# Cosine attention and a gated MLP on one core: three-chunk score visits, a Newton norm for one unit, and a new order of early loads

## The chip, the cores and the metric

The kernel runs on one core of one Trainium2 chip. The metric is the device time of one execution in microseconds (us). Profiles are of single executions; a core has five engines with a queue each: TensorE (PE, with its weight loads as PEld), VectorE (DVE), ScalarE (ACT), GpSimd (POOL) and SyncE (SP, which here only issues DMAs).

## What is computed

The reference, cut to what matters (8 batches, 12 heads, 448 positions, head width 64; 3584 tokens, model width 768, hidden width 2048):

```python
q_n = q / (norm(q, axis=-1) + 1e-06)
k_n = k / (norm(k, axis=-1) + 1e-06)
scores = matmul(q_n, k_n.T) / tau              # tau = 0.1
attn = exp(scores - max(scores)); attn = attn / sum(attn)
x = matmul(attn, v)                            # heads joined: 3584 x 768
h = x @ w_in                                   # 768 x 2048
g = h * cos(h)
out = g @ w_out                                # 2048 x 768
```

All inputs and the output are float32 in DRAM; the kernel multiplies in bfloat16.

## The kernel before, in words

**Units and groups.** The work is cut into 16 units of six heads (two units are one batch) and 48 groups of two heads (three groups are one unit, six a batch, PB = 6). Group g belongs to unit u = g // 3.

**One unit's inputs** (`load` L647, `load_v` L655, `copy_v` L665, `norms` L933). SP issues the DMAs of k and q (both into a `raw` buffer, two buffers, units alternate) and of v (`vin`). `square` (L680) squares 112x1024 elements a group, on POOL unless `PLAN` (L14) or the rule in `norms` names ACT or DVE; `reduce` (L696) sums on DVE; `rnorm` (L704) makes 1/norm on ACT as exp(-0.5 ln x), for one group in units 0 and 1 and for three groups at once afterwards; `scale` (L714) multiplies k and q by it, on POOL except for group 0. `copy_v` casts v to bfloat16, on DVE for units 0 and 1 and on POOL afterwards.

**One group's attention.** `transposes` (L730) turns the normed k and q so that the head width lies on partitions: on TensorE and then a DVE copy for groups below `BYPE` = 9, by a DMA transpose from SP above. `scores` (L756) makes one of four chunks of scores: two matmuls, one a head, each on half of the array's rows, into one of two PSUM tiles SC0 and SC1 (two banks each); ACT takes the exponential of the chunk (PX). `both` (L950) puts two chunks together; such a run of score matmuls, between matmuls that use all rows, is called a visit here. `attend` (L776) multiplies PX by v into the PSUM tile AV, and DVE takes the reciprocal of the sums (`rcp`) and scales (`xs`, both read AV). xs is transposed into xT: by DMA, or, for the groups in `XPE` (batch 0 and the last group of each batch), by TensorE into the AV tile (XP) and a DVE copy.

**The MLP.** `m1` (L815) is the first projection of one batch: eight steps of 24/2 matmuls of 448 columns, into SC0, SC1 and AV in the order of `TURN`; the last step lies in AV. ACT takes the cosine (as a sine, for which it loads another table, 1.28 us each way) and DVE multiplies (gT). `m2_emit` (L866) is the second projection in halves of 16 matmuls of 384 columns, into PSUM tiles PO and PO2 in turn, then a DVE copy (osb) and an output DMA. PO2 is also the tile of the transposes (TP).

**What sets the order.** The code only lists operations with costs; a planner (`play` L218, `arrange` L176) plays them through and writes each engine's fixed order; `pick` (L264) chooses for TensorE among the first three groups of stream A and the head of stream B, which holds M2 alone and fills. Operations with a bias over 500 (the weight loads) are taken by their due times `DUE` (L522), W1.0 at -20, W1.1 at 10, W2.0 to W2.3 at 20, 24, 28, 32. W1 is loaded in halves and W2 in quarters by DMAs that POOL issues (`load_w1` L906, `load_w2` L912). Where TensorE would idle early, dummy matmuls on zeros (L919) are put in.

**The main sequence** (L981 to L1041): norms and transposes of group 0; groups 0 to 5 by `pair` (L956); loads of unit 2, W2.0 and W2.1, the norms of unit 2, loads of unit 3 after W1.1 has landed; transposes of groups 6 to 8; `m1(0)`; then groups 6 to 47 by `pair`, with `m1(b)` and its M2 after group 6(b+1)+1 (after group 12 for b = 1), and `m1(7)` and the rest of M2 at the end. M2 of the next to last batch is listed with eight halves only, the rest after the last attend.

## Time and profile before

| what | value |
|---|---|
| median of 6 runs | 434.8 us (433.85 to 435.63) |
| the profiled execution | 435.49 us |
| its span in the profile | 433.6 us |
| granted TensorE clock | 1.0 throughout |
| ACT exponentials (L767) | 192, 165.0 us busy, 914 ns each |
| M2 (L877), M1 (L826), AV (L785), scores (L762) on PE | 816+64+16, 480+288, 1536, 384 matmuls |
| POOL squares (L693) and scales (L719) | 42 and 47, 1906 and 1903 ns each |
| DMA queues: SP and ACT / POOL | 55.6% / 7.9% of 16 engines' span |

How to read it: a matmul's end is modelled, so that pieces of work are best measured from one start to the next; the projection's 24 matmuls take 4.54 us in the chain of waits. The first 36 us hold the attention of batch 0, 36.5 to 56.4 the first projection, 56.4 to 90.9 attention with the first M2; from 109.5 on attention with M2 and projections follow in turn, and from 397.6 only M2 is left.

### The profile page before, as it was taken

To read this page: it belongs to the slowest core of one execution; us is meant where nothing else is said; L and a number is where in the kernel's file an instruction comes from. 1 tells how busy PE (TensorE), PEld (TensorE's weight loads), DVE (VectorE), ACT (ScalarE), POOL (GpSimd) and SP (SyncE) were. 2 spreads that over 40 slices of the span, in tenths; PEclk is the share of its full clock that TensorE was granted. 3 is DMA by queue.
4 is the path that set the end of the run, shared out by engine and by line. 5 is a ranking of instruction groups with operands and counts; after the bars stand their busy time and mean duration, and the time that the engine had idled before them with its cause. 6 is when DMAs were issued, how large, how long until landed. Compare 5 with 4: busy or idle time off the path is not lost.

```text
span 433.6 us, 8767 instructions
## 1 busy us (share of the span) xinstructions
PE 417.9 (96%) x3756; PEld 225.8 (52%) x3756; DVE 212.9 (49%) x297; ACT 264.6 (61%) x319; POOL 192.8 (44%) x118
## 2 busy tenths in 40 slices
PE   7889999999899999999999989999999999999996
PEld 2455545544555545555555545555555545655663
DVE  5776646464636356534853366424853344335221
ACT  3887386874777647784677637774677547734000
POOL 3995167912876546932496056921596000000000
PEclk9999999999999999999999999999999999999999
DMA  9999997598179596648757694759857102200322
GB/s 230 264 246 213 241 273 160 143 234 211 33 176 244 105 266 188 107 117 224 180 118 115 164 232 95 122 133 211 176 113 134 48 0 59 59 2 0 100 81 77
DMA packets 94631, 63.87 MB, mean 147 GB/s; under 512 B 55040, under 2 KB 89600, under 8 KB 94592
## 3 DMA queue, kind: packets, MB, share of 16 engines
q1 hardware_dynamic: 90064, 56.16, 55.6%
q0 software_dynamic: 3680, 6.29, 7.9%
q10 hardware_dynamic: 848, 0.86, 0.7%
q8 instruction: 30, 0.49, 0.5%
q14 instruction: 9, 0.07, 0.1%
HBM read 45.61 MB, written 11.01 MB: 131 GB/s over the span
## 4 chain that ended last, share of the span: by engine, by line
PE 79%; ACT 7%; issue 5%; POOL 3%; DMA 3%; DVE 2%; SPq 0%; POOLq 0%; ACTq 0%
PE PO L877 29%; PE SC L826 16%; PE AV L785 10%; PE AV L826 10%; PE SC L762 9%; ACT PX L767 6%; DMA raw<-in_q_dram 3%; PE SC L877 2%; POOL sq L693 2%; POOL qks L719 1%; PE AV L877 1%; DVE n L700 1%; DVE gT L842 1%; ACT cosb L840 0%; PE PO L745 0%
## 5 line engine op out<-in xcount | busy, mean ns | idle before, releaser
L767 ACT ACTIVATE PX<-SC 112x896 bf16<-112x896 f32 x192 | 165.0, 914 | 44.3 <-PE SC L762 43.8
L877 PE MATMUL PO<-W,gT 128*128 128x384 bf16 x816 | 148.6, 326 | 0.0
L693 POOL TENSOR_TENSOR sq<-raw 112x1024 bf16<-112x1024 f32 x42 | 79.4, 1906 | 103.4 <-DMA raw<-in_q_dram 103.4
L877 PEld LDWEIGHTS PO<-W,gT 128*128 128x128 bf16 x816 | 73.0, 97 | 56.8 <-issue 13.1
L719 POOL TENSOR_TENSOR qks<-raw,rn 112x1024 bf16<-112x1024 f32 x47 | 88.4, 1903 | 25.0 <-ACT rn L711 25.0
L826 PE MATMUL SC<-xT,W 128*128 128x448 bf16 x480 | 95.5, 352 | 1.0 <-ACT PX L767 1.0
L842 DVE TENSOR_TENSOR gT<-SC,cosb 128x896 bf16<-128x896 f32 x40 | 43.5, 1091 | 54.9 <-ACT cosb L840 54.6
L840 ACT ACTIVATE cosb<-SC,cst 128x896 f32<-128x896 f32 x40 | 40.2, 1007 | 48.4 <-PE SC L826 43.4
L826 PEld LDWEIGHTS SC<-xT,W 128*128 128x128 bf16 x480 | 46.6, 98 | 43.9 <-issue 1.4
L700 DVE TENSOR_REDUCE n<-sq 112x16 f32<-112x1024 bf16 (+1 forms) x49 | 58.1, 1191 | 16.8 <-POOL sq L693 12.0
L826 PE MATMUL AV<-xT,W 128*128 128x448 bf16 x288 | 58.7, 352 | 2.4 <-ACT cosb L840 1.2
L762 PE MATMUL SC<-qkT 64*128 64x448 bf16 x384 | 55.5, 355 | 5.0 <-ACT PX L767 2.2
L785 PEld LDWEIGHTS AV<-va,PX 112*128 112x128 bf16 x1536 | 49.4, 97 | 15.6 <-issue 11.3
L785 PE MATMUL AV<-va,PX 112*128 112x65 bf16 x1536 | 54.8, 193 | 0.9 <-ACT PX L767 0.8
L884 DVE COPY osb<-PO 128x384 f32<-128x384 f32 x51 | 28.2, 553 | 39.2 <-PE PO L877 39.2
L840 ACT ACTIVATE cosb<-AV,cst 128x896 f32<-128x896 f32 x24 | 24.2, 1007 | 33.9 <-PE AV L826 33.8
L826 PEld LDWEIGHTS AV<-xT,W 128*128 128x128 bf16 x288 | 27.5, 98 | 30.1 <-ACT cosb L840 2.6
L794 DVE RECIPROCAL rcp<-AV 112x8 f32<-112x8 f32 x48 | 10.0, 207 | 66.5 <-PE AV L785 66.5
L842 DVE TENSOR_TENSOR gT<-AV,cosb 128x896 bf16<-128x896 f32 x24 | 26.2, 1090 | 18.7 <-ACT cosb L840 18.6
L795 DVE TENSOR_TENSOR xs<-AV,rcp 112x512 bf16<-112x512 f32 x48 | 33.2, 692 | 2.0
L762 PEld LDWEIGHTS SC<-qkT 64*128 64x128 bf16 x384 | 13.3, 94 | 37.6 <-ACT PX L767 17.4
L667 POOL CAST va<-vin 112x1536 bf16<-112x1536 f32 x14 | 20.5, 1465 | 11.1 <-DMA vin<-in_v_dram 7.7
(34 smaller groups left out, 121.9 us busy)
## 6 DMA issues: line engine op xcount, KB each, us to landing
vin<-in_v_dram SPq DMA_DIRECT2D x16, 672.0 KB, 10.9
raw<-in_k_dram SPq DMA_DIRECT2D x12, 672.0 KB, 8.4
raw<-in_q_dram SPq DMA_DIRECT2D x12, 672.0 KB, 10.7
W<-in_moe_w_in_dram POOLq DMA_DIRECT2D x2, 1536.0 KB, 14.6
W<-in_moe_w_out_dram POOLq DMA_DIRECT2D x4, 768.0 KB, 21.4
raw<-in_k_dram SPq DMA_DIRECT2D x12, 224.0 KB, 7.1
out_dram<-osb SPq DMA_DIRECT2D x7, 336.0 KB, 2.8
out_dram<-osb SPq DMA_DIRECT2D x8, 288.0 KB, 2.7
```

The source lines that it names most:

```text
L693: pool(lambda e, x=x, y=y: e.tensor_tensor(y, x, x, ALU.mult), src_, dst, 0.1 + n * 1.78e-3, label="sq%d.%d" % (u, p))
L700: dve(lambda e, w=w: e.tensor_reduce(out=n2v[i][:, 2 * p : 2 * p + 2, w], in_=sqv[p][:, :, w, :], axis=mybir.AxisListType.X, op=ALU.add), ...
L719: f = lambda e, s0=s0, s1=s1: e.tensor_tensor(qksv[i][:, p, s0:s1, :, :].rearrange("p s h d -> p h s d"), rawv[i][:, h, s0:s1, :], bass.AP ...
L762: t = e.matmul(SCv[z][:, a, 0:S], qkT[k].ap()[r, NP * c : NP * c + 128], qkT[k].ap()[r, S : 2 * S], start=True, stop=True)
L767: act(lambda e: e.activation(PXv[j][:, c, 0 : 2 * S].rearrange("p (a s) -> p a s", a=2), SCv[z][0:NP, :, 0:S], ACT.Exp, scale=1.0 / TAU), ...
L785: t = e.matmul(AVv[:, a, DV * x : DV * x + n], PXv[j][:, c, k : k + 128], vav[i][:, NJ * (2 * p + a) + c, 0:n], start=(c == 0), stop=(c == ...
L795: dve(lambda e: e.tensor_tensor(xsv[y].rearrange("p x h d -> p h x d"), AXv[:, :, :, 0:D], bass.AP(rcp[y], 0, [[NS, NP], [NJ, 2], [1, NJ], ...
L826: t = e.matmul(ph[:, a, 0:S], W1v[:, c, 128 * n : 128 * n + 128], xTv[b % 2][:, c, :], start=(c == 0), stop=(c == NKC - 1))
L840: act(lambda e, ph=ph, cz=cz: e.activation(cosv[cz], ph[:, :, 0:S], ACT.Sin, bias=cst.ap()[:, 0:1], scale=1.0), names(gi) + ["cst0"], [("c ...
L842: dve(lambda e, ph=ph, cz=cz, gi=gi: e.tensor_tensor(gTv[:, 2 * gi : 2 * gi + 2, S * (b % 2) : S * (b % 2) + S], ph[:, :, 0:S], cosv[cz], ...
L877: r = e.matmul(po[:, 0:HW], gTv[:, y, col : col + 128], W2v[:, y, HW * hf : HW * hf + HW], start=(y == 0), stop=(y == NF - 1))
L884: dve(lambda e, po=po, o=o, hf=hf: e.tensor_copy(osb[o].ap()[:, HW * hf : HW * hf + HW], po[:, 0:HW]), keys, [("osb", o, hf)], HW, label=" ...
```

## The change

The visits of groups 12 to 47 hold three chunks that follow one another across groups: twelve chunks of three groups make four visits. The chunks' PSUM tile rotates over AV, SC0 and SC1. A projection stands after the second visit of a batch's first three groups. XP moves from the AV tile to PO or PO2. Unit 2's loads wait for the landing of W1.0; its squares are all on POOL, and its inverse norms are found by three Newton steps (two small DVE and twelve small POOL operations a call, two calls) in place of Ln and Exp on ACT. Its norms and transposes are listed behind `m1(0)`. Both W1 loads are issued behind sq0.2, all W2 loads behind scale1.2. Group 3's squares (unit 1) go from POOL to ACT; Ln and Exp of units 0 and 1 get a due time 4 us earlier. Groups 9 to 11 are transposed on TensorE, into AV. DVE copies v of units 0 and 1 in three pieces; group 0's two reductions become one. In the planner, a DMA from POOL is taken to start later, M2 of a second half may start while the first waits, the trials differ, and M2 is listed as five or six halves after each projection and the rest after XP.

The core of the diff:

```diff
-    "sq": ["AD", "A", "P", "P", "P", "P"],
+    "sq": ["AD", "A", "P", "A", "P", "P"],
...
-            if fill and left[fill[0].idx] == 0:
-                o = fill[0]
-                t = max(free["PE"], ready_at[o.idx])
+            o = None
+            for x in fill[:9]:
+                if left[x.idx] == 0 and (x is fill[0] or x.group != fill[0].group):
+                    y = max(free["PE"], ready_at[x.idx])
+                    if o is None or y < t - 0.15:
+                        o, t = x, y
+            if o is not None:
...
-                queue[e].append([o, o.start + (1.7 if e == "POOL" else 1.1), o.bulk + 0.02])
+                queue[e].append([o, o.start + (5.0 if e == "POOL" else 1.1), o.bulk + 0.02])
...
-    BYPE = 9
+    BYPE = 12
...
+    NEWTON, STEPS = (2,), 3
+    SQ2 = "PPP"
+    SOON = -4.0
+    BYHEAD = False
+    BEHIND0 = "sq0.2"
+    LASTW = "scale1.2"
+    BEFORE2 = "W1.0"
+    G3 = 12
+    KEEP = (0, 1, 0, 1, 0, 1, 0)
+    SPREAD = (5, 6, 6, 6, 6, 6, 6)
+    AT, AT1 = 1, 1
...
+        if u in NEWTON:
...
+            small(lambda e: e.tensor_scalar(m, m, 1e-12, None, ALU.add), km, km, dve)
+            small(lambda e: e.tensor_scalar(y.bitcast(I32), m.bitcast(I32), -0.5, 1597463007.0, ALU.mult, ALU.add), km, ky, dve)
+            for x in range(STEPS):
+                small(lambda e: e.tensor_tensor(t, y, m, ALU.mult), km + ky, kt)
+                small(lambda e: e.tensor_tensor(t, t, y, ALU.mult), kt + ky, kt)
+                small(lambda e: e.tensor_scalar(t, t, -0.5, 1.5, ALU.mult, ALU.add), kt, kt)
+                small(lambda e: e.tensor_tensor(y, t, y, ALU.mult), kt + ky, ky)
+            return
...
+        if g >= PB + UP - 1:
+            views, keys = (AVt, AVt), ("AV", "AV")
...
     def scores(g, c):
-        j, k, z = g % 2, g % UH, (c + 1) % 2
+        j, k, q = g % 2, g % UH, NJ * g + c
+        name, bank = PHs[1 + (c + 1) % 2 if g < G3 else q % 3]
...
+        keys, view = ["PO"], POv
+        if g >= 2 * PB - 1:
+            keys, view = [(["PO"], POv), ([("TP", 0), ("TP", 1)], TPv)][nhalf[0] % 2]
+            nhalf[0] += 1
...
+        if g >= 2 * PB - 1:
+            m2_emit(max(0, len(m2_queue) - KEEP[g // PB - 1]))
...
+    def visit(g, n):
+        q = NJ * g + 3 * n
+        for x in range(q, q + 3):
+            scores(x // NJ, x % NJ)
...
+    P.order_only(find(BEHIND0), find("W1.0"))
+    P.order_only(find(BEHIND), find("W1.1"))
+    last_scale = find(LASTW)
     for p in range(UP):
         load(2, p, p + 1)
+        if BEFORE2:
+            after(P.ops[-1], find(BEFORE2))
     load_w2(0)
+    P.order_only(last_scale, P.ops[-1])
...
+    for g in range(G3, NG, 3):
+        for n in range(4):
+            if n < 3:
+                ahead(g + n)
+            grouped(visit, g, n)
+            if n < 3 and g + n > PB:
+                attend(g + n - 1)
+            if n == 0:
+                values(g)
+            if g % PB == 0 and g > PB and n == (AT if g > 2 * PB else AT1):
+                project(g // PB - 1, g)
```

`ahead`, `values` and `project` hold what `pair` and the main loop held before: the next unit's norms and DMA transposes, the cast of v with the loads of unit 4, and a projection with the loads and M2 that follow it.

## The prediction, made before the changed kernel was run

> **What bounds the kernel now.** The page comes first: TensorE's share of the span and the chain of waits.
>
> ```profile
> PE 417.9 (96%) x3756; PEld 225.8 (52%) x3756; DVE 212.9 (49%) x297; ACT 264.6 (61%) x319; POOL 192.8 (44%) x118
> ...
> q0 software_dynamic: 3680, 6.29, 7.9%
> ...
> PE 79%; ACT 7%; issue 5%; POOL 3%; DMA 3%; DVE 2%; SPq 0%; POOLq 0%; ACTq 0%
> ```
>
> TensorE holds 79% of the chain and no other engine more than 7%. Next, busy time by stretch tells where it is the bound: two five-microsecond slices near the start, one projection, and the attention stretch after it.
>
> ```profile
> 55.00:60.00 5.00, 4.42 (x26) 1.99 (x24) 3.14 (x3) 3.13 (x4) 3.66 (x2) 1.00 1.11 297
> 60.00:65.00 5.00, 4.50 (x52) 2.41 (x54) 1.90 (x3) 5.00 (x7) 2.96 (x3) 1.00 1.11 256
> ...
> 145.01:164.50 19.49, 18.89 (x100) 9.52 (x98) 10.19 (x11) 8.51 (x9) 9.39 (x6) 1.00 0.95 215
> 164.50:193.76 29.26, 29.26 (x345) 16.32 (x345) 14.35 (x24) 23.48 (x30) 19.72 (x11) 1.00 0.59 130
> ```
>
> Columns: stretch, length, then busy time and count on PE, PEld, DVE, ACT and POOL, the clock, DMA share, GB/s. From 164.5 TensorE has no idle time at all (29.26 of 29.26), with ACT at 80%. So a stretch of attention is shortened only by giving TensorE less to do. What it does there is seen in the timeline of TensorE, one period:
>
> ```profile
> 221.19 0.55 PE L762 MATMUL SC<-qkT 64*128 64x448 bf16 x4
> 221.67 2.12 PE L877 MATMUL PO<-W,gT 128*128 128x384 bf16 x12
> 223.73 0.55 PE L762 MATMUL SC<-qkT 64*128 64x448 bf16 x4
> 224.21 1.14 PE L785 MATMUL AV<-va,PX 112*128 112x65 bf16 x32
> 225.19 0.81 PE L877 MATMUL PO<-W,gT 128*128 128x384 bf16 x4
> 225.94 0.55 PE L762 MATMUL SC<-qkT 64*128 64x448 bf16 x4
> ```
>
> I read starts, since ends are modelled. A visit of two score chunks lasts 0.48 (221.19 to 221.67). Its four matmuls run two at a time on halves of the array's rows; 448 columns cost 0.189 each in the projection (24 in 4.54 us in the chain), so 0.38 is work and 0.10 is not. Twelve M2 matmuls take 2.06 (221.67 to 223.73); in the tail 72 take 11.70, that is 1.95 for twelve, so another 0.11 lies between M2 and the next visit. One visit costs about 0.21 beyond its work.
>
> Early in the run TensorE does idle, and fills holes with dummy matmuls (L919):
>
> ```profile
> 56.92 2.12 PE L877 MATMUL PO<-W,gT 128*128 128x384 bf16 x12
> 58.88 0.54 PE L919 MATMUL PO<-zt 128*128 128x448 bf16 x2
> 60.20 0.36 PE L762 MATMUL SC<-qkT 64*128 64x448 bf16 x2 [0.78 <-ACT PX L767]
> 60.50 0.36 PE L919 MATMUL PO<-zt 128*128 128x448 bf16 x1
> 61.01 0.36 PE L762 MATMUL SC<-qkT 64*128 64x448 bf16 x2
> ...
> 62.11 0.82 PE L877 MATMUL PO<-W,gT 128*128 128x384 bf16 x4
> ```
>
> From 58.88 to 62.11 only three single-chunk visits of 0.30 (the third at 61.82) are real work: 2.3 us lost. A second hole lies at 89.38 to 90.94 (1.5), a third at 109.8 to 111.0 (1.2, score bank still read by a delayed gT product).
>
> [...] the DMA share is 1.0 or above until 65 us, whichever queue issues, so moving a load moves only its turn.
>
> **Part by part.**
>
> *Three-chunk visits, groups 12 to 47.* 36 groups now have 72 visits and will have 48. 24 x 0.21 = -5.0 us. Both ends: zero if the visits cannot come in time, -5.8 at 0.24 a visit.
>
> They add a wait. Chunks now rotate over AV, SC0 and SC1, and the first chunk of every visit lies in the AV bank that the AV product also uses. So a visit waits until xs of the last product has read AV, and the product waits for the first exponential of the visit. Prices from the timeline by engine:
>
> ```profile
> 171.21 0.55 PE L762 MATMUL SC<-qkT 64*128 64x448 bf16 x4
> 171.61 1.73 ACT L767 ACTIVATE PX<-SC 112x896 bf16<-112x896 f32 x2 [0.78 <-PE SC L762]
> 171.69 1.02 PEld L785 LDWEIGHTS AV<-va,PX 112*128 112x128 bf16 x32 [0.37 <-DVE osb L884]
> ...
> 172.87 0.21 DVE L794 RECIPROCAL rcp<-AV 112x8 f32<-112x8 f32 x1 [1.58 <-PE AV L785]
> 173.11 0.69 DVE L795 TENSOR_TENSOR xs<-AV,rcp 112x512 bf16<-112x512 f32 x1
> ```
>
> Visit to first exponential 0.40, one exponential 0.865, AV start to the end of xs 2.11. A visit whose product needs its first chunk repeats after 0.40 + 0.865 + 2.11 + 0.1 = 3.5; the third of four, whose product needs two new chunks, after 4.35; the fourth, with no product behind it, after three exponentials, 3.05. Four visits: 14.4. After a projection the last product sits in AV, so the first visit comes some 2.4 late (gT ends at 166.8, M1 at 164.5). From projection to projection, eight visits: 2.4 + 4.35 + 3.05 + 3.5 + 3.5 + 4.35 + 3.05 + 3.5 + 2.1 until SC0 is read = 29.8. TensorE's own demand with 100 M2 matmuls, as now, is 29.3 - 4 x 0.21 = 28.5, and 30.4 with all 112 of a batch; the tail holds 12.5 halves (200 matmuls from 397.6), seven of them the last batch's, so 5.5 halves can be drawn forward. The wait is thus covered by M2, barely. Behind a waiting visit on TensorE stands the next M2, which the planner can put first; behind a late xs on DVE stand osb copies and a 1.21 reduction. I charge +1.0 for all six stretches; bounds 0 and +10 (below).
>
> *XP to PO or TP banks, M2 spread, M2 allowed to start in the other bank.* XP's work stays (0.2 each, one a batch); its copy of 0.39 borrows an M2 bank while the other fills. Zero. Allowing the second half's M2 while the first waits is what fills 58.88 to 62.11: -2.0 of 2.3. If W2 has not landed it is 0. The four W2 issues (0.78 each) now follow scale1.2 in a row, from about 28.5, and the last comes near 31 instead of 32.16; queue q0 needs 7.9% of 433.6 = 34 us of all engines for both weights either way, so I take their landing as unchanged. At 90 and 110 I take -0.5 each, of 1.5 and 1.2.
>
> *First attention (ACT-bound, exponentials 10.04 to 35.49).* sq1.0 goes from POOL (1.9) to ACT (1.06), where 1.53 of idle time before 15.80 covers it. POOL's scales come up to 1.9 earlier; W2.0 and W2.1 (1.51 of issue at 26.10) leave scale1.2's way, which started at 27.64 though its square sums were ready before 26.3; Ln and Exp of the norms go ahead of exponentials. ACT's idle times that this can remove are 0.61, 0.79 and 0.40; I take -0.7, bounds 0 and -1.8. The value copies in three pieces, 0.58 each at the reduction's rate, cost DVE two more starts: zero.
>
> *Unit 2.* Its raw loads wait for W1.0 to land, which was 10.65 + 17.0 = 27.7 and comes sooner without them beside it, about 24. Then they share engines with W1.1: 1.34 MB, at 230 GB/s 5.9 alone, about twice that shared, so 30 to 36. POOL then has three squares (5.7), a DVE reduction (1.2), twelve Newton operations [...], two scales (3.8): transposable by 50 at worst. The first projection runs to about 55.7 and hides this; the cover of 6 us is gone at 0.75 us per operation. The second chain and scale2.2 end near 55. ACT loses a square, Ln and Exp (1.66 together) and can load its table earlier, but the first sine waited for TensorE (41.09), so zero. Behind unit 2 on POOL stand sq3.0 and sq3.1, whose data landed only at 56.3: free unless Newton runs over. Unit 3's transposes (groups 9 to 11) go from DMA to TensorE: 3 x 0.40 (45.07 to 45.46 for one, about) = +1.2.
>
> Sum: -5.0 + 1.0 - 2.0 - 1.0 - 0.7 + 1.2 = -6.5. The profiled execution took 435.49 (span 433.6, 1.9 around it), 0.69 above the median of 434.8. So its counterpart is 429.0, and the median **428.3**.
>
> **Rivals.**
> - *Everything hides*: -5.0, -1.8, -2.3, -1.5, -1.2, the 1.23 that M1 waits at 257.6 as well, +1.2: -11.8, 423.0. For: every one of these is idle time in the trace. Against: each is someone's wait, and the next wait is close.
> - *Only the visits pay*: the early holes stay because W2 or the last gT sets them, Newton operations cost 0.75 and push sq3 by 1 to 2: -5.0 + 1.2 + 1.5 = -2.3, 432.5. For: DMA is full until 65.
> - *Slower: the AV bank becomes the loop.* If two reductions of 1.21 fall before rcp or xs in each stretch, the 29.8 becomes 32.2 against 30.4 of demand: 1.8 idle x 6 = +10.8 in place of 1.0, so 434.8 - 7.5 + 10.8 = 438.1. It decides from 31.6 a stretch. For: DVE runs 14.35 of 29.26 there, and today's visits never touch AV. Against: ACT and DVE orders are planned, and M2 covers 0.6.
> - *The change does not do what it says*: the planner splits the visits again; within 0.2% of now.
>
> **Numbers.** Forecast (426 to 431) 0.42; everything hides 0.18; only the visits 0.17; slower 0.19; none 0.04. No change means within 0.2%, 0.9 us, about what this measurement can tell. Faster 0.77, same 0.04, slower 0.19. Range 422.0 to 434.5: it leaves out some 0.16 above and 0.04 below.
>
> **What would show it.** Six score matmuls per visit, and visits about 0.67 to 0.69 long; 29.2 between projections with 104 to 112 M2 matmuls in it, or PE idle before L762 put down to DVE xs (then the slower rival); no L919 at 59 to 62; POOL's small operations at 0.15 to 0.3 and scales of unit 2 done before 55. I am wrong if TensorE idles behind AV for more than 1.3 us a stretch, or if unit 2's transposes come after M1 has ended.

## The result and the profile after

The changed kernel takes 435.22 us (median of 35 runs, 433.11 to 438.87); the kernel before takes 434.54 (72 runs, 432.46 to 437.69). The ratio is 1.0021, with a 95% interval of 1.0008 to 1.0034: slower by about 0.2%, 0.9 us, where 6.5 us less were forecast, and outside the range by 0.7. The profiled execution, 433.11 us with a span of 431.3, is the fastest of the 35; a second one of the same kernel, 434.26 with a span of 432.5, lies nearer to the median, and both are used below. The profiles alone would make the changed kernel the faster one: the profiled execution of the kernel before (435.49) was above its median, both of the changed kernel are below theirs. So the result is read from the medians, and the traces are read for where time is lost and gained.

One thing sets the runs of the changed kernel apart. Of the 36 that are listed with their clock, 24 have a mean granted clock of 0.996 or less and a median of 436.1, the other twelve 0.998 or more and a median of 434.1. Of the kernel before's 161 runs in the jobs of the experiments, 19 are of the first kind.

The page first, with TensorE's share and the chain of waits:

```profile
PE 417.7 (97%) x3779; PEld 228.9 (53%) x3779; DVE 216.9 (50%) x307; ACT 262.0 (61%) x317; POOL 197.8 (46%) x142
...
q0 software_dynamic: 3680, 6.29, 7.8%
...
PE 86%; ACT 5%; DVE 3%; POOL 3%; issue 1%; DMA 1%; DVEq 0%
```

TensorE still bounds, now with 86% of the chain. The busy time by slice (columns as before: slice, length, busy time and count of PE, PEld, DVE, ACT and POOL, clock, DMA share, GB/s):

```profile
55.00:60.00 5.00, 4.04 (x36) 2.26 (x34) 2.65 (x4) 3.96 (x4) 4.27 (x11) 1.00 1.10 247
60.00:65.00 5.00, 4.63 (x32) 2.12 (x32) 3.35 (x4) 3.65 (x6) 5.00 (x4) 1.00 0.77 209
143.08:161.70 18.62, 18.52 (x98) 9.45 (x99) 10.23 (x10) 7.49 (x8) 8.88 (x5) 1.00 0.97 212
161.70:192.60 30.90, 30.83 (x356) 17.46 (x355) 13.95 (x23) 22.94 (x30) 19.64 (x11) 1.00 0.58 132
```

Between 55 and 65 TensorE isn't busier than before (8.67 us of 10 against 8.92), and GpSimd (POOL) is busy for 9.27 of the 10 where it was 6.62. The attention stretch is full, as before, and longer since it holds more M2 matmuls. TensorE's timeline there, one group of three:

```profile
263.25 0.36 PE L817 MATMUL AV<-qkT 64*128 64x448 bf16 x2
263.45 0.54 PE L817 MATMUL SC<-qkT 64*128 64x448 bf16 x4
263.92 1.47 PE L937 MATMUL PO<-W,gT 128*128 128x384 bf16 x8
265.43 1.14 PE L840 MATMUL AV<-va,PX 112*128 112x65 bf16 x32
...
270.53 0.36 PE L817 MATMUL AV<-qkT 64*128 64x448 bf16 x2
270.73 0.54 PE L817 MATMUL SC<-qkT 64*128 64x448 bf16 x4
271.21 0.82 PE L937 MATMUL PO<-W,gT 128*128 128x384 bf16 x4
271.91 1.14 PE L840 MATMUL AV<-va,PX 112*128 112x65 bf16 x32
```

The visits hold three chunks and last 0.68 (270.53 to 271.21), as forecast. But a product (AV) no longer follows a visit: it follows M2. Eight M2 matmuls at the tail's rate of 0.1625 are 1.30; the product starts 1.51 after they do (263.92 to 265.43), and in the shorter piece 0.70 after four that cost 0.65.

In the second profile of the same kernel, TensorE's timeline where the first projection hands over to attention again:

```profile
57.19 0.55 PE L799 MATMUL PO<-ident,qks 112*128 112x112 bf16 x8 [0.66 <-DVE gT L905]
57.68 0.55 PE L817 MATMUL SC<-qkT 64*128 64x448 bf16 x4
58.16 0.82 PE L937 MATMUL PO<-W,gT 128*128 128x384 bf16 x4
61.74 0.55 PE L799 MATMUL AV<-ident,qks 112*128 112x112 bf16 x8 [2.75 <-POOL qks L767]
62.22 0.36 PE L817 MATMUL SC<-qkT 64*128 64x448 bf16 x2
62.52 1.37 PE L937 MATMUL PO<-W,gT 128*128 128x384 bf16 x4
```

The fourth line is the transposing of group 8, unit 2's last, and it stands 2.75 us for GpSimd's scale (1.33 in the first profile). Four M2 matmuls behind it take 1.30 (62.52 to 63.82) instead of 0.65: the clock was lowered. In slices of five microseconds:

```profile
55.00:60.00 5.00, 3.33 (x29) 1.60 (x26) 2.34 (x3) 3.95 (x4) 4.27 (x12) 1.00 1.11 266
60.00:65.00 5.00, 3.26 (x20) 1.23 (x21) 2.15 (x3) 1.50 (x2) 5.00 (x3) 0.77 0.80 213
65.00:70.00 5.00, 5.00 (x55) 2.55 (x54) 3.22 (x5) 4.77 (x8) 3.43 (x4) 0.89 1.05 268
```

In slices of one microsecond the clock is 0.83, 0.50, 0.50, 0.50 and 0.97 from 62 to 67, with TensorE busy throughout: that loses another 1.7, as 0.23 x 5 + 0.11 x 5 does. A loss of 1.7 in 432 is a mean clock of 0.996, what most runs of this kernel show. Two waits for gT, 0.59 and 0.66, which the first profile doesn't have, come ahead of the one for group 8.

I call the time from the start of one projection to that of the next a stretch, and take 0.1625 for each M2 matmul off its length, since the two kernels place M2 differently. So cleared, the first stretch is 38.8 in the kernel before and 43.6 in the second profile of the changed one. Of these 4.8, 1.46 is work moved forward (two score chunks and a product more) and 1.4 the transposes of groups 9 to 11, which went by DMA before: some 1.9 are lost. The second stretch falls from 35.0 to 32.0, so by 1.6 without the moved work. The next four are 32.0, 31.5, 32.6 and 31.5 before and four times 31.3 after; from the third projection to the end the changed kernel gains 1.9, of which 1.1 is a single wait before a projection (1.23 at 258.8 in the kernel before).

### The profile page after: what moved, and what is told of

The parts are those of the page before. It is cut to its first block, busy times and chain, and to the rows that moved or that the text cites. A ratio compares the mean times of both kernels' runs of the same rounds, so it can differ in the third digit from the quotient of the medians.

```text
span 431.3 us, 8851 instructions
## 1 busy us (share of the span) xinstructions
PE 417.7 (97%) x3779; PEld 228.9 (53%) x3779; DVE 216.9 (50%) x307; ACT 262.0 (61%) x317; POOL 197.8 (46%) x142
## 4 chain that ended last, share of the span: by engine, by line
PE 86%; ACT 5%; DVE 3%; POOL 3%; issue 1%; DMA 1%; DVEq 0%
PE PO L937 32%; PE SC L889 19%; PE AV L889 11%; PE AV L840 11%; PE SC L817 6%; ACT PX L822 4%; PE AV L817 3%; DVE n L728 1%; POOL qks L767 1%; PE AV L937 1%; PE SC L937 1%; DMA raw<-in_q_dram 1%; DVE qks L767 1%; PE PO L870 1%; PE AV L799 0%
## 5 line engine op out<-in xcount | busy, mean ns | idle before, releaser
L937 PE MATMUL PO<-W,gT 128*128 128x384 bf16 x832 | 152.2, 327 | 0.0
L822 ACT ACTIVATE PX<-SC 112x896 bf16<-112x896 f32 x144 | 123.2, 917 | 8.5 <-PE SC L817 8.2
L937 PEld LDWEIGHTS PO<-W,gT 128*128 128x128 bf16 x832 | 74.2, 98 | 62.7 <-issue 20.0
L822 ACT ACTIVATE PX<-AV 112x896 bf16<-112x896 f32 x48 | 44.0, 917 | 47.3 <-PE AV L817 47.3
L903 ACT ACTIVATE cosb<-SC,cst 128x896 f32<-128x896 f32 x40 | 40.1, 1006 | 51.0 <-PE SC L889 51.0
L889 PEld LDWEIGHTS SC<-xT,W 128*128 128x128 bf16 x480 | 46.3, 98 | 43.6 <-issue 1.6
L728 DVE TENSOR_REDUCE n<-sq 112x16 f32<-112x1024 bf16 x48 | 57.7, 1211 | 7.0 <-POOL sq L722 4.0
L889 PE MATMUL AV<-xT,W 128*128 128x448 bf16 x288 | 58.5, 352 | 0.7
L840 PE MATMUL AV<-va,PX 112*128 112x65 bf16 x1536 | 56.2, 193 | 1.2 <-ACT PX L822 0.6
L817 PE MATMUL SC<-qkT 64*128 64x448 bf16 x288 | 41.9, 352 | 2.0 <-ACT PX L822 1.1
L905 DVE TENSOR_TENSOR gT<-AV,cosb 128x896 bf16<-128x896 f32 x24 | 26.2, 1090 | 15.1 <-ACT cosb L903 14.8
```

The costliest lines, as they stand in the source:

```text
L728: dve(lambda e, o=o, hs=hs: e.tensor_reduce(out=n2v[i][:, o, :], in_=sqv[p][:, hs[0] : hs[-1] + 1, :, :], axis=mybir.AxisListType.X, op=AL ...
L817: t = e.matmul(bank[:, a, 0:S], qkT[k].ap()[r, NP * c : NP * c + 128], qkT[k].ap()[r, S : 2 * S], start=True, stop=True)
L822: act(lambda e: e.activation(PXv[j][:, c, 0 : 2 * S].rearrange("p (a s) -> p a s", a=2), bank[0:NP, :, 0:S], ACT.Exp, scale=1.0 / TAU), [n ...
L840: t = e.matmul(AVv[:, a, DV * x : DV * x + n], PXv[j][:, c, k : k + 128], vav[i][:, NJ * (2 * p + a) + c, 0:n], start=(c == 0), stop=(c == ...
L889: t = e.matmul(ph[:, a, 0:S], W1v[:, c, 128 * n : 128 * n + 128], xTv[b % 2][:, c, :], start=(c == 0), stop=(c == NKC - 1))
L903: act(lambda e, ph=ph, cz=cz: e.activation(cosv[cz], ph[:, :, 0:S], ACT.Sin, bias=cst.ap()[:, 0:1], scale=1.0), names(gi) + ["cst0"], [("c ...
```

## The experiments

All times are medians, and the ratio is to runs of the kernel before in the same job.

| run | us | ratio | 95% interval |
|---|---|---|---|
| e1_again | 435.90 | 1.0042 | 1.0022 to 1.0062 |
| e2_after_two | 440.90 | 1.0151 | 1.0105 to 1.0196 |
| e3_before_three | 441.66 | 1.0171 | 1.0140 to 1.0202 |
| e4_after_race | 435.22 | 1.0027 | 1.0007 to 1.0047 |
| e5_one_chain | 435.67 | 1.0034 | 1.0014 to 1.0054 |
| e6_act_norm | 435.89 | 1.0043 | 1.0024 to 1.0061 |
| e7_one_step | 433.60 | 0.9988 | 0.9971 to 1.0005 |
| e8_loads | 431.31 | 0.9944 | 0.9922 to 0.9967 |
| e9_hold_before | 440.23 | 1.0139 | 1.0116 to 1.0163 |
| e12_no_hold_ln | 436.63 | 1.0052 | 1.0030 to 1.0073 |
| e13_step_start | 430.52 | 0.9925 | 0.9904 to 0.9947 |
| e14_no_hold_two | 436.87 | 1.0073 | 1.0047 to 1.0100 |
| x1_order_hold | 439.09 | 1.0116 | 1.0073 to 1.0159 |
| x2_order_no_hold | 431.51 | 0.9920 | 0.9892 to 0.9948 |
| x3_start_pool | 432.85 | 0.9948 | 0.9929 to 0.9967 |
| x4_pool_one | 433.17 | 0.9950 | 0.9933 to 0.9967 |

### The changed kernel again, and the visits alone

The changed kernel as it is:

> The changed kernel again, for a second profile of it. The one at hand took 433.11, the fastest of its 35 runs (median 435.22), so it hides what a usual run loses. Theory A (steady part all right, the opening decides): the stretch from the third projection's start to the end stays at 288.2 within 0.3, and what differs lies before 145. Theory B (the AV wait of the three-chunk visits is met late in a usual run): PE idle before L817 or L840 of 1 us or more after 145, put down to DVE xs or ACT PX, and the stretch 1 to 2 longer. Median 435 under both.

It gave 435.90, and the profile with the wait of 2.75 shown above. From the third projection to the end both profiles take 288.2, as Theory A has it; but the opening, on which it puts the difference, is the shorter one here (first projection at 35.6 instead of 36.9), and the first stretch is what is longer (59.2 instead of 55.2).

The changed kernel with two-chunk visits everywhere:

```diff
-    G3 = 12
+    G3 = 48
...
+        if g % PB == 1 and g > 2 * PB:
+            project((g - 1) // PB - 1, g - 1)
```

> The changed kernel with visits of two chunks in SC0 and SC1 for groups 12 to 47 again; the projections stay where they are (after six chunks and the same attends). The prediction's price, 24 visits at 0.21: 5 us slower than the changed kernel, about 440. Theory A, from the profile (a half stretch of three groups has 1.47 of overhead against 1.57 before, because AV now starts after M2 and not after a visit and waits 0.21 for its exponential): 1 to 2 slower, 436 to 437. Theory B (visits cost more in waits than they save): equal or faster, 433 to 435.

440.90, 5.0 more than with three chunks, about the prediction's price. But the later stretches, cleared of M2, are 31.7 to 31.8 against 31.3: 0.5 a batch, and 2.3 from the third projection to the end. The rest lies in the first two (46.0 and 34.0 against 43.6 and 32.0), in the first of which the planner had also listed the work in another order.

The kernel before with three-chunk visits:

```diff
+        name, bank = PHs[1 + (c + 1) % 2 if g < 2 * PB else q % 3]
...
-    for g in range(PB, NG):
+    for g in range(PB, 2 * PB):
...
+    for g in range(2 * PB, NG, 3):
+        for n in range(4):
...
+            grouped(visit, g, n)
```

> The kernel before with three-chunk visits alone for groups 12 to 47 (and a projection after six chunks for batch 1 as for the others), all else as it was. The prediction's price: 429.5. Theory A: 1 to 2 us faster than before, 433. Theory B: 434.5 or slower.

441.66. Its first stretch is 45.7 where the kernel before has 38.8, with 80 dummy matmuls in the run instead of 48. So this edit made that kernel slower, most of all in the early order that was planned with it. Its later stretches are no shorter either: 33.6 and then three times 31.9, where the kernel before has 32.0, 31.5, 32.6 and 31.5. Neither run isolates the visits. Over all runs a regular stretch with two-chunk visits takes 31.2 (e9_hold_before), 31.5 (the kernel before) or 31.8 (e2, e14), and one with three-chunk visits 31.3 or 31.9: what else the order does weighs as much as the size of the visits.

### The opening

In the first profile of the changed kernel the first exponential starts at 11.82, 1.8 later than before, because VectorE's (DVE) first scale, two instructions from 7.33 on, took 2.99 us instead of 1.29. GpSimd's square of group 2 had started at 7.88, between them. A run in which that square waits for the scale:

```diff
+    after(find("sq0.2"), find("scale0.0"))
```

> The changed kernel with POOL's square of the third group held until the DVE has scaled the first group. In its profile the DVE's second piece of that scale took until 10.3 and not 8.7, beside POOL's square that had started at 7.88, and the first exponential came at 11.82 and not at 10.04. If the order of these two (set by when the load lands) is what costs: first exponential near 10.0, 1.0 to 1.8 us faster than the changed kernel, median 433.5 to 434.2, and a narrower spread. If it is covered later by waits for loads: 435 as it is.

The scale takes 1.29 and the first projection starts at 35.9 instead of 36.9, but the time is 435.22 and the wait for group 8 is 2.75. Settling the opening doesn't bring the forecast back.

### Unit 2: its chain and its loads

GpSimd in the changed kernel (first profile), unit 2's squares, the last of its first chain, and its scales:

```profile
35.19 1.89 POOL L722 TENSOR_TENSOR sq<-raw 112x1024 bf16<-112x1024 f32 x1 [5.26 <-DMA raw<-in_q_dram]
40.08 1.90 POOL L722 TENSOR_TENSOR sq<-raw 112x1024 bf16<-112x1024 f32 x1 [3.00 <-DMA raw<-in_q_dram]
44.98 1.89 POOL L722 TENSOR_TENSOR sq<-raw 112x1024 bf16<-112x1024 f32 x1 [3.01 <-DMA raw<-in_q_dram]
...
50.49 0.22 POOL L753 TENSOR_SCALAR lnn<-lnn 112x32 f32<-112x32 f32 x1
50.79 0.25 POOL L754 TENSOR_TENSOR rn<-lnn,rn 112x32 f32<-112x32 f32 x1
51.12 1.90 POOL L767 TENSOR_TENSOR qks<-raw,rn 112x1024 bf16<-112x1024 f32 x1
...
58.32 1.90 POOL L767 TENSOR_TENSOR qks<-raw,rn 112x1024 bf16<-112x1024 f32 x1
```

Two things make the last scale end at 60.2: the raw values arrive until 45, and two chains of twelve operations follow, 0.30 to 0.33 from one start to the next. In the second profile W1's first half lands at 26.2 instead of 24.7; the squares then start at 37.0, 41.9 and 46.8 and the last scale ends at 61.6. What the raw values share the DMA engines with shows by queue, from 30 to 45 us of the first profile (packets, MB, share of the 16 engines; q0 carries the weights, q1 nearly all else):

```profile
q0 software_dynamic: 1428, 2.17, 79.1%
q1 hardware_dynamic: 1434, 1.37, 33.7%
```

The two queues moved nearly the same number of packets, of 1.52 KB on average in q0 and 0.96 in q1, so that the raw values got 91 of 239 GB/s and each group's 448 KB took 4.9 us. W1's second half landed at 33.5 and W2's last piece at 55.3, so that q0 was busy all the while. Three runs shorten the chains or bring the loads forward. The chain made one for all three groups:

```diff
-    norms(2, 0, 2)
+    norms(2, 0, 3)
     transposes(PB)
     transposes(PB + 1)
-    norms(2, 2, 3)
```

> The three groups of unit 2 go through one Newton chain instead of two (groups 6 and 7, then group 8): some 12 small GpSimd operations fewer, started to started 0.30 to 0.33 us each, but the first scale of unit 2 has to wait for the third sum. Theory A (unit 2's chain on GpSimd ends too late, and TensorE's wait for group 8's scale in the second stretch, 1.3 to 2.8 us with the granted clock lowered after it, is where the visits' gain of about 1.9 us goes): the last scale of unit 2 ends some 3 us earlier (near 57 instead of 60.2), the wait of group 8's transposes shrinks to under 1 us, the stretch from the first to the second sin stage loses 1.5 to 2.5 us, the time is 433 to 434. Theory B (the stretch is long because six groups are transposed in it and the listed order of the fillers has changed, whatever GpSimd does): the wait moves, the stretch keeps its 58 to 59 us, the time is 435.

The wait shrinks to 0.90 and the scales end at 58.8, later than Theory A had it. The first stretch, cleared, falls from 43.6 to 40.0, but the second grows from 32.0 to 35.6: in its projection VectorE stands 2.02 for a GpSimd square before a sum, the product gT listed behind that sum is late, and TensorE waits 2.07. The time stays at 435.67. A gap closed; another of the same kind opened.

One Newton step instead of three:

```diff
-    NEWTON, STEPS = (2,), 3
+    NEWTON, STEPS = (2,), 1
```

> One Newton step instead of three in unit 2's norm: two of the three steps of each chain are left out, 8 small GpSimd operations a chain, so that the norm of these three groups is only roughly found. Theory A: the two chains end together about 4 to 5 us earlier (the last scale of unit 2 near 55.5), the wait of group 8's transposes is gone, 1.5 to 3 us come back: 432 to 434. Theory B: the wait is gone but the stretch keeps its length, 435. What the run measures beside that is the price of a Newton step: 8 operations by 0.30 to 0.33 us in each chain.

433.60, as Theory A has it, and the wait for group 8 is gone. But TensorE now stands 2.92 for a gT product of the first projection. VectorE's timeline there:

```profile
45.46 0.17 DVE L748 TENSOR_SCALAR n<-n 112x32 f32<-112x32 f32 x1
45.66 0.18 DVE L749 TENSOR_SCALAR rn<-n 112x32 int32<-112x32 int32 x1
45.78 1.09 DVE L905 TENSOR_TENSOR gT<-SC,cosb 128x896 bf16<-128x896 f32 x1
48.23 1.22 DVE L728 TENSOR_REDUCE n<-sq 112x16 f32<-112x1024 bf16 x1 [1.35 <-POOL sq L722]
49.36 1.08 DVE L905 TENSOR_TENSOR gT<-SC,cosb 128x896 bf16<-128x896 f32 x1
50.36 1.02 DVE L748 TENSOR_SCALAR n<-n 112x16 f32<-112x16 f32 x1
51.41 1.82 DVE L749 TENSOR_SCALAR rn<-n 112x16 int32<-112x16 int32 x1
53.15 1.08 DVE L905 TENSOR_TENSOR gT<-AV,cosb 128x896 bf16<-128x896 f32 x1
```

The two opening operations of the second chain are half as large as those of the first and take 1.02 and 1.82 instead of 0.17 and 0.18, while GpSimd scaled. In x1 below the first of them takes 1.61 and ends at 55.09, where GpSimd's two scales ran from 51.29 to 55.05. That VectorE stood for GpSimd is my reading of these times; what held it isn't shown. The test is to move those operations to GpSimd, TensorE's, ScalarE's and SP's orders staying as they are:

```diff
-            small(lambda e: e.tensor_scalar(m, m, 1e-12, None, ALU.add), km, km, dve)
-            small(lambda e: e.tensor_scalar(y.bitcast(I32), m.bitcast(I32), -0.5, 1597463007.0, ALU.mult, ALU.add), km, ky, dve)
+            small(lambda e: e.tensor_scalar(m, m, 1e-12, None, ALU.add), km, km)
+            small(lambda e: e.tensor_scalar(y.bitcast(I32), m.bitcast(I32), -0.5, 1597463007.0, ALU.mult, ALU.add), km, ky)
```

> As the run with one Newton step (433.6 when it ran), the hold in place and two of the three steps left out again, but the two opening operations of each chain (adding the small constant, and the first guess on the integer view) are on GpSimd instead of VectorE; TensorE's, ScalarE's and the DMA queues' orders are the same. In that run the second chain's two operations, 112x16 each, took 1.02 and 1.82 us on VectorE while GpSimd scaled (0.17 and 0.18 for the first chain's with GpSimd between operations), the product behind them was late and TensorE stood 2.92 us for it. Theory A (VectorE's small operations wait until GpSimd's large one is through): the 2.92 us are gone or under 0.6, the first sin stage lasts 18.8 to 19.2 us instead of 21.6, the time is 431 to 432. Theory B (the product is late for the third sum, which VectorE has to wait for ahead of it, 1.35 us): 1 to 2 us of the wait stay, the time is 433.

430.52, by the ratios 0.6% or 2.7 us less, and the 2.92 are gone; the first projection lasts 18.8 us instead of 21.6. That is Theory A, with a time 0.5 below its range. VectorE's third sum waits only 0.39 for GpSimd here instead of 1.35, so a part of Theory B isn't excluded. With two Newton steps left out this isn't the changed kernel's full computation.

Unit 2's loads not held behind W1:

```diff
-    BEFORE2 = "W1.0"
+    BEFORE2 = ""
```

> Only the hold on unit 2's loads is taken away: they are issued ahead of W1's landing, as in the kernel before. The Newton chains stay. Theory A, in its first form (the loads are what makes the chain late: GpSimd's three squares of unit 2 stood 5.3, 3.0 and 3.0 us for them): the squares run back to back, the last scale of unit 2 ends 5 us earlier or more, the wait of group 8's transposes is gone: 432 to 434. Theory A, in its second form (the chain of small operations is what makes it late, the loads only move the waiting): the last scale ends less than 2 us earlier, the time is 434.5 to 435.5. Theory B: 435 with the wait gone. A cost of its own would be W1 landing later, since the two would share the DMA engines: the first sin stage then starts after 36.

431.31, ratio 0.9944: faster than both kernels. GpSimd:

```profile
28.25 1.93 POOL L722 TENSOR_TENSOR sq<-raw 112x1024 bf16<-112x1024 f32 x1
33.99 1.89 POOL L722 TENSOR_TENSOR sq<-raw 112x1024 bf16<-112x1024 f32 x1 [3.81 <-DMA raw<-in_q_dram]
39.37 1.89 POOL L722 TENSOR_TENSOR sq<-raw 112x1024 bf16<-112x1024 f32 x1 [3.49 <-DMA raw<-in_q_dram]
...
52.57 1.90 POOL L767 TENSOR_TENSOR qks<-raw,rn 112x1024 bf16<-112x1024 f32 x1
56.42 3.74 POOL L722 TENSOR_TENSOR sq<-raw 112x1024 bf16<-112x1024 f32 x2 [1.94 <-DMA raw<-in_q_dram]
```

The last scale ends at 54.5 instead of 60.2 and group 8 is transposed without a wait. The squares don't run back to back; Theory A's first form was right in the last scale and the wait, not in that; the time is 0.7 below its range. W1 isn't later for it: the first projection starts at 35.7 (35.6 with the hold, second profile). From there to the second projection 54.7 us pass instead of 59.2, and after it both take about the same (338.3 and 337.7 to the end of the span). The first stretch is the whole difference from that profile.

### The hold by itself

In that run the planner had also listed TensorE's work in another order. Two runs add or take away the hold after the planning, each engine's order staying that of the kernel compared with. First the kernel without the hold (431.31), the hold added:

```diff
     P.arrange()
+    for n, o in enumerate(o for o in P.ops if o.label.startswith("load u2 p")):
+        o.start = max(o.start, find("W1.0").start + 0.01 * (n + 1))
+        after(o, find("W1.0"))
```

> The kernel without the hold (431.31 when it ran), every engine in the same order, but with the hold added after the planning: unit 2's raw loads are issued at W1's first half's landing, near 24.7, instead of 8.6 to 17.7. Theory A (the hold itself): the squares of unit 2 come 6 to 7 us later again, group 8's transposes stand for the last scale, 434.5 to 436. Theory B (the order planned around it): 431 to 432.

439.09, worse than either theory had it. VectorE shows why:

```profile
37.30 1.22 DVE L728 TENSOR_REDUCE n<-sq 112x16 f32<-112x1024 bf16 x1 [6.71 <-POOL sq L722]
38.43 0.38 DVE L874 COPY xT<-PO 128x448 bf16<-128x448 bf16 x1
```

A sum of unit 2 is listed ahead of a copy of batch 0's attention result (xT). It waits 6.71 for the late square, the copy behind it is late, TensorE stands 5.22 for the copy, the clock is lowered (0.88 from 40 to 60 us, 0.992 over the 436.3 of the span), and the first projection starts at 42.9 instead of 35.7. After that the two kernels' stretches are alike.

Then the changed kernel (435.22), the hold taken away:

```diff
     P.arrange()
+    w1 = find("W1.0")
+    for o in [o for o in P.ops if o.label.startswith("load u2 p")]:
+        o.deps = [d for d in o.deps if d[0] is not w1]
```

> The changed kernel (435.2), every engine in the same order, with the hold taken away after the planning. Theory A (the hold itself): the last scale of unit 2 ends near 53 instead of 60, TensorE's wait of 1.3 to 2.8 us for it is gone, 431.5 to 433. Theory B (the order): 435. Something of both would be 433 to 434.

431.51, ratio 0.9920. The wait for group 8 is still 1.24: the last scale ends at 58.5, not at 53 as expected. The third square starts at 38.5 here, but GpSimd's first chain only at 45.5, after standing 5.10 for VectorE's opening operations, which this order lists behind three products of the projection. The clock stays at 1.00. The first projection starts at 35.3 and the first stretch is 55.1: against the second profile of the changed kernel (35.6 and 59.2) the stretch is shorter, against the first (36.9 and 55.2) the opening. The opening is lost without the hold too (e12_no_hold_ln below), so what part of it in the first profile is the hold's isn't known.

As a ratio to the kernel before, the hold costs 1.0021 - 0.9920 = 1.0%, 4.4 us, in the changed kernel's order, and 1.7%, 7.5 us, in the other. So Theory A stands in this: it is the hold, whatever the order. A part of it comes with the clock. A mean of 0.996 or less shows in 24 of the changed kernel's 36 runs but in one of the 6 without the hold; in the other order it shows in none of the 10 runs without the hold and in all 6 with it. When the loads are issued shows on SP's queue, first in the changed kernel, then without the hold:

```profile
24.74 0.31 SPq L676 DMA_DIRECT2D raw<-in_k_dram  x1
...
27.10 0.46 SPq L676 DMA_DIRECT2D raw<-in_q_dram  x1
```

```profile
8.69 1.66 SPq L676 DMA_DIRECT2D raw<-in_k_dram  x1
...
16.34 0.46 SPq L676 DMA_DIRECT2D raw<-in_q_dram  x1
```

The same hold put into the kernel before:

```diff
         load(2, p, p + 1)
+        after(P.ops[-1], find("W1.0"))
```

> The kernel before with one part of the change alone: its loads of unit 2 wait for the landing of W1's first half. Norm on ScalarE, two-chunk visits and the rest stay as they were. Theory A (the hold by itself costs what the changed kernel lost, since everything of unit 2 stands behind its raw values): the squares of unit 2 start some 5 us later, its groups are transposed inside the first projection and so hold up its end, the first stretch grows by 2 to 4 us: 436.5 to 438.5. Theory B (the hold costs only together with the Newton chains on GpSimd): 434 as before. The first half of W1 may land up to 1 us earlier, which takes that much off the first sin stage's start under both.

440.23, against theory B, but more than A expected: this kernel also loses the opening (its first scale takes 2.99) and starts its first projection at 40.3, with the clock lowered in the opening (0.992 over the span; four score matmuls from 11.26 on take 0.86, where such a visit takes 0.48), so that of its 6 us only the sign is evidence. Its first stretch grows by 2.6, as A has it.

### What the norm, the visits and the small operations are worth without the hold

Unit 2's norm as Ln and Exp, without the hold:

```diff
-    NEWTON, STEPS = (2,), 3
+    NEWTON, STEPS = (), 3
...
-    BEFORE2 = "W1.0"
+    BEFORE2 = ""
...
-    norms(2, 0, 2)
+    norms(2, 0, 3)
...
-    norms(2, 2, 3)
```

> The changed kernel without the hold (431.31 when it ran) and with unit 2's norm as Ln and Exp on ScalarE in place of the Newton chains; transposes stay behind the first projection. It asks what the Newton chains by themselves are worth. Theory A (they pay nothing now that the loads come early: ScalarE's two operations of 0.33 and 0.24 us come with a table load of 1.28 us that has to be made anyway between the sin stage and the next exponential): 431 to 432, and the last scale of unit 2 ends near 61 only if the norm waits for the end of the sin stage, which would bring a wait of 1 to 3 us on TensorE back and 433 to 434. Theory B (the chains spare ScalarE two table loads inside the sin stage, 2.6 us, that TensorE would wait for): 433.5 to 435.

436.63, by the ratios 1.1% or 4.7 us above the run with the chains. ScalarE makes the norm only at 59.56, behind the last sine, and GpSimd scales from 60.25 on: the late norm that Theory A named, at the price of Theory B. The opening lost 1.8 of them (first projection at 37.5 instead of 35.7, the first scale 2.99), so about 3 are left, and the first stretch is 3.1 longer: in this order the Newton chains do pay once their data is early.

The other way round, with unit 2 wholly as in the kernel before (a square, Ln and Exp on ScalarE, transposes in the first projection, no hold), and the rest of the change kept:

```diff
-    NEWTON, STEPS = (2,), 3
-    SQ2 = "PPP"
+    NEWTON, STEPS = (), 3
+    SQ2 = "PPA"
...
-    BEFORE2 = "W1.0"
+    BEFORE2 = ""
...
+    norms(2, 0, 3)
...
+    for g in range(PB, PB + UP):
+        transposes(g)
```

> Unit 2 goes back to the order of the kernel before: its loads aren't held behind the first half of W1, one of its squares is on ScalarE, its norm is Ln and Exp on ScalarE with the table loads, and its three groups are transposed inside the first projection. Three-chunk visits and W2's place in the queue stay. Theory A: the early loss of about 2.4 us is gone and the visits' 1.9 us stay: 431 to 433, faster than both kernels. Theory B (the visits' own early order of fillers costs as much, as it did when the visits alone were put into the kernel before): the first stretch is again 4 to 6 us longer, the time is 435 to 441.

435.89, a miss: I had hoped for the fastest version. Behind its first projection and in its second TensorE stands for gT, 2.32 and 2.29, and each time VectorE had a sum of the next unit ahead of that product, waiting 2.82 for ScalarE's square and 2.24 for GpSimd's.

Two-chunk visits without the hold:

```diff
-    G3 = 12
+    G3 = 48
...
-    BEFORE2 = "W1.0"
+    BEFORE2 = ""
```

> The changed kernel without the hold and with two-chunk visits from group 12 on. With the early loss out of the way this is the price of the visits by themselves. Theory A: 0.3 us a batch, 1.8 to 1.9 us in all, so 433.2. The prediction's own sum for the visits (5.0 less 1.0 for the waits on the bank): 435.3. The same edit in the kernel with the hold cost 5 us, of which 4 lay in its first two stretches: if that is the edit's own effect on the early order it comes back here, 435 to 436 with the first stretch longer than 56 us.

436.87, by the ratios 5.6 above the kernel with three chunks, though the first stretch is 55.6, not above 56: above all three expectations. Cleared of M2, the third to sixth stretches are 31.7 to 31.8 against 31.3 to 31.4; the second is 34.0 against 32.0, with waits of 0.76 for gT and 1.45 for a transpose by DMA ahead of the third projection. The first stretch is 1.6 longer, with waits of 0.82 for W2 and 0.73 for GpSimd's scale. So it is 0.5 a batch where the order is regular; how much of the first two stretches is the visits' and how much the order's stays open.

The two opening operations on GpSimd, as in the diff shown above, without the hold and with all three steps; and the same with one step:

> The kernel without the hold, all three Newton steps in place, with the two opening operations of each chain on GpSimd instead of VectorE; TensorE's, ScalarE's and the DMA queues' orders are the same. In the kernel without the hold the second chain's two took 1.61 and 1.83 us on VectorE beside GpSimd's scales, but TensorE stood only 0.35 us for the product behind them. Theory A (what VectorE loses counts only as far as TensorE waits for it): 0.3 us faster than without it, 430.5 to 431.3. Theory B (the 3 us of VectorE delay more than the trace shows in one place): 429 to 430.

> As x3, with one Newton step instead of three (two of the three steps of unit 2's norm are left out): 16 small operations fewer on GpSimd, 5 us of its time, TensorE's order the same. Theory A (with the loads early the chain ends in time and its length costs nothing): the same as x3 within 0.5 us. Theory B (the chain's length still counts): 1 us or more faster than x3.

432.85 and 433.17, with the kernel before at 434.99 in that job: ratios 0.9948 and 0.9950, against 0.9944 without either, no difference that can be told. With early loads, neither VectorE's 3.4 us nor the length of the chain shows in the time. W2's new place in the queue wasn't tried by itself.

## Why the prediction was wrong, step by step

- **Unit 2, costed at nothing: the step that failed.** The prediction put the raw values at "30 to 36", everything "transposable by 50 at worst" and the last scale "near 55". They let the squares start at 35.2, 40.1 and 45.0 (37.0, 41.9 and 46.8 in the second profile), and the last scale ended at 60.2 (61.6). The mis-sized term is the transfer: "about twice that shared" is half the rate beside W1's second half alone. The raw values got 91 of 239 GB/s, with the weights' packets the larger (1.52 KB against 0.96), and when W1's second half had landed at 33.5, W2's four pieces, issued from 26.88 on, kept that queue busy. So "moving a load moves only its turn" was wrong as well: it moved this one beside other loads. No run moves W2 or changes the packets; that the hold costs the time is shown by taking it away. The small operations took 0.30 to 0.33 from start to start, 7.2 to 7.9 us over the 24 of both chains, a price that the trace of the kernel before doesn't show. The cover was then gone. In the changed kernel the wait for group 8 shows it, and most runs (24 of 36) have a lowered clock besides, which the second profile shows right behind it; with one Newton step (e7) and in the other order (x1) the delay travels through VectorE, where the prediction looked for nothing, having listed only what stands behind unit 2 on GpSimd. Measured: +4.4 us for the hold, all its effects together.
- **Holes at 58.88, "-2.0 of 2.3".** M2 does run in that place, but the wait for group 8 took it: 1.33 or 2.75 idle in two profiles, with the lowered clock on top in one. The hole moved to another owner. The sign named for it, unit 2's transposes coming after the first projection (M1) has ended, tells nothing: they do here (55.5, 57.2, 60.4) and in e8, without the hold and 4 us faster (54.6, 56.3, 57.3). Only what the third one waits for differs. The holes at 90 and 110, "-0.5 each", are closed: TensorE's waits of 1.02 and 1.21 there are in neither profile.
- **Visits, "24 x 0.21 = -5.0" and "+1.0".** The price of a visit is right, the saving isn't. Three groups now take 14.79 with 52 M2 matmuls (263.25 to 278.04), before 14.24 with 48; less 0.65 for the four, 14.14 against 14.24. Two visits fewer save 0.42 of that, but 0.32 is paid again ahead of the three products, which followed a visit before at no price of their own and now follow M2: 0.21 once, where the profile has TensorE's weight load waiting for the exponential, and 0.05 twice. Over six batches that is 3.8, where the "+1.0" was to cover the waits that the visits add. Measured 0.2 a batch against the kernel before (31.3 and 31.5), in place of 0.7; against two-chunk visits in the changed kernel 0.5; and the other way in e3 (31.9 and 31.5). So no single price of the visits is shown. The bank AV was no loop: TensorE waits for xs once in the first profile (1.29 at 143.08) and not at all in the second.
- **First attention, "-0.7".** Right where the first scale takes 1.29 (projection at 35.6 and 35.9 instead of 36.5), lost where it takes 2.99 (36.9).
- **Transposes of groups 9 to 11, "+1.2", and W2's landing, 0.** Those of groups 9 to 11 take 0.49, 0.40 and 0.50 (from 69.39, 73.23 and 77.08 on in the first profile), 1.4 in all, so the size is nearly right; TensorE waits for W2 nowhere in the two profiles of the changed kernel. W2 mattered all the same, as what the raw values shared the engines with.
- **The rivals.** The slower one, the AV bank, has the right sign for the wrong reason. With the hold away (0.9920 of 434.54, 431.1) the kernel still lies 2.8 above the forecast. The wait of 1.24 that is left for group 8 and the visits' missing 1 to 3 us are the parts known; they aren't a closed sum.

## What to carry to other kernels

Before a load is held back for another, list all that share the DMA engines while it catches up, with the size of their packets (here the held load got 91 of 239 GB/s), and follow what waits for its last byte through every engine's listed order, not only through the engine that reads it. A sum whose input may be late shouldn't stand ahead of a product or copy that TensorE needs (in x1 the sum waited 6.71 and TensorE 5.22). And where a planner writes the order, test an edit with the order kept as well as replanned: x1 and x2 tell the hold from the order in two runs, which no replanned run did.

## What the runs showed of the hardware

- VectorE's two-input scale and its small one-input operations took longer beside a GpSimd instruction: 2.99 instead of 1.29, and 1.02, 1.82 (e7) and 1.61 (x1) instead of 0.16 to 0.26. In the opening the two cases go with the start of GpSimd's square: with it 0.35 (e12), 0.49 (e9) or 0.55 (first profile) after the scale's start, the scale took 2.99; from 0.60 on (e13) it took 1.29, and the square up to 2.44 instead of 1.9.
- Two DMA queues moved nearly packet for packet in two windows, though the packets differed in size: 1428 and 1434 packets with W2 beside the raw values (30 to 45 us of the first profile, 91 of 239 GB/s for these), and 315 and 315 in the kernel before from 20 to 24 us, beside W1 (75 of 235). From 45 to 55 us of the first profile it was 807 and 1326.
- An idle time of 2.75 us (second profile) was followed by half the clock for some 3.4 us, an estimate from the 1.7 us lost there. Behind one of 2.07 (e5) twelve projection matmuls took 3.84 instead of 2.27, and about one of 5.22 (x1) the clock was lowered too (0.88 from 40 to 60 us). But with 2.75 in e4 and 2.32 in e6 the mean over the span is 1.00, and behind 2.92 in e7 the twelve matmuls took 2.26. Their length alone doesn't decide, and what does stays open.
